# Turning the second chunk's y with VectorE and transfers instead of TensorE, and loading it first in the phase

## The chip, the cores and the metric

One NeuronCore of a Trainium2 chip. The metric is the device time of one execution in microseconds: the median of the runs, and for questions of where time goes, one execution that the hardware profiler recorded.

## The reference

An input x of 2048 tokens with 512 features goes through a normalization. Its result feeds two branches, whose outputs are multiplied and added to x:

```python
xn = _layernorm(x, axis=-1)
s = _A_ref(xn, A_wqkv, A_wo)                       # attention: 32 heads of 16, each query sees the 256 keys up to itself
g = _silu(_B_ref(xn, B_w1, B_b1, B_w2, B_b2))      # y = layernorm(xn); gelu(y @ w1 + b1) @ w2 + b2, with F = 1792
return x + s * g
```

Everything is float32.

## The kernel before

Matrix products are made of three passes: each operand is split into a high part that TensorE multiplies in one pass and a low rest, and high x high, high x low and low x high are added. A split is a cast (mostly on ScalarE) and a subtraction (on VectorE).

The kernel has two parts. Up to about 426 us it does the attention, with other work filled in between. Its results, not yet divided by the sums of the softmax, go to memory in `oT_d`, and the sums with them, as row `DH` of each head. Ten of the fourteen tiles of the hidden layer of the first 512 tokens are also made there, 2, 3 and 6 to 13; the last eight go to memory in `h_d`. Tiles 0 and 1 follow at its end.

The second part, which the change touches, runs over four chunks of 512 tokens. For chunk 0 (`c == 0` in the loop `for c in range(2)`) it runs over the 14 tiles of the hidden layer, in the order 2, 3, 0, 1, 4, 5, 6 to 13, by a counter `i`. For each tile, `activate` applies the gelu on ScalarE (`g`) and splits the result into `gh` and `gl`; `project` lets TensorE multiply these with w2 into `acc`, 12 matmuls a tile, of which every third reads `gl`. There are two buffers each of `gh` and `gl`. Tiles 4 and 5 are multiplied out here (`h`); the later ones come back from `h_d` (`hr`).

Beside this run over the tiles:

- the sums: `fetch_sums` loads them as `den`; VectorE inverts them in four parts; one transfer stores them (`rden_d`), and `load_o` brings back, for each of four groups, the attention (`or`) and the inverses spread over the partitions (`w<-rden_d` in the profile, since a w2 tile is used for them). VectorE multiplies the two and `split_o` splits the product (`ohl`);
- y of chunk 1: its four tiles of normalized x are loaded from `xn_d`, normalized once more (statistics on VectorE, a power on GpSimd, and here the normalization on VectorE), and, after the last `project`, turned by TensorE.

`end_chunk` adds the bias, applies the silu, and multiplies `ohl` with wo (`s`, 24 matmuls in the profile for each pair of token tiles). In chunk 0 it calls `between`, which puts the turning of y for chunk 1 before `s` of tiles 0 and 2: `y_transpose` makes four transposes of 128x128 into PSUM for each of four feature tiles, and splits the result into `yy`, the input of the hidden layer. Chunks 2 and 3 have their y turned in another way already: `turn_y` lets VectorE transpose a 128x512 tile in blocks of 32x32 and stores it in `z_d`, and `fetch_y` reads it back with four transfers for each feature tile, in runs of 32 elements, which puts the blocks in their places.

All transfers are issued by SyncE, one after the other, each waiting for what it needs; a wait holds up those behind it. Where `nc.sync.on` is set, they are issued in the order of the code; otherwise a scheduler may move them. Instructions of each other engine run in the order of the code. A transfer uses one of eight completion counters in turn, and its issue waits until the last one on its counter has landed.

Of the kernel before, what the change touches and what calls it, by code (L numbers as in the profile page):

```python
# [9 lines left out]
F32 = mybir.dt.float32  # L10
# [7 lines left out]
S, D, H, DH, WIN, F = 2048, 512, 32, 16, 256, 1792  # L18
P = 128
NCH = S // 512  # L20
NKB = S // P
KT = D // P
# [28 lines left out]
def mixer_kernel(ctx, tc, x, wqk, wv, wo, w1, b1, w2, b2, out):  # L51


    nc = SimpleNamespace(**{name: Ordered(tc, name) for name in ("tensor", "vector", "scalar", "gpsimd", "sync")})
# [3 lines left out]
    t2 = ctx.enter_context(tc.tile_pool(name="t2", bufs=5))  # L58
# [10 lines left out]
    def split(dst_hi, dst_lo, src, eng=None):  # L69

        (eng or nc.scalar.copy)(dst_hi, src)
        nc.vector.tensor_sub(dst_lo, src, dst_hi.bitcast(F32))
# [4 lines left out]
    def load(pool, tag, src, name, shape=(P, 512)):  # L77
        t = pool.tile(list(shape), F32, tag=tag, name=name)
        nc.sync.dma_start(t, src)
        return t  # L80
# [83 lines left out]
    def load_x(c, pools, name):  # L164
        return [load(*pools[i % len(pools)], x[512 * c + P * i: 512 * c + P * (i + 1), :], f"{name}_{c}_{i}")
                for i in range(4)]
# [19 lines left out]
    w_d = {"w1": dram.tile([P, NF * 512], F32, name="w1_d"), "w2": dram.tile([P, NF * 512], F32, name="w2_d"),  # L186
           "wo": dram.tile([P, 4 * 512], F32, name="wo_d")}
    g_d = dram.tile([NF, P, 512], F32, name="g_d")
    z_d = dram.tile([2, 4, P, 512], F32, name="z_d")
    mT_d = dram.tile([NQ, NCH, 32, P], F32, name="mT_d")  # L190


# [392 lines left out]
    mlp = {}  # L585
# [42 lines left out]
    def fetch(kind, f):  # L628

        nc.sync.dma_start(w_part(kind, 1, f).bitcast(F32), w_d[kind][:, 512 * f: 512 * (f + 1)])  # L630
# [9 lines left out]
    def y_steps(a, b):  # L640
        run(mlp["ln"][a:b])

    def y_transpose(c, kt, ps=None):
        ts = mlp["y"]
        if ps is None:
            ps = ps_yt.tile([P, 512], F32, tag="b", name=f"yt_{c}_{kt}")
        for i in range(4):
            nc.tensor.transpose(ps[:, P * i: P * (i + 1)], ts[i][:, P * kt: P * (kt + 1)], ident)
        split(mlp["yy"][0][kt], mlp["yy"][1][kt], ps)

    def hidden_mm(ps, f, k):
        kt, (a, b) = k // 3, PASSES[k % 3]
        nc.tensor.matmul(ps, w1_part(a, f)[:, P * kt: P * (kt + 1)], mlp["yy"][b][kt],
# [217 lines left out]
    wos = cp.tile([P, 2, 4, 512], F32R, name="wos")  # L871
    for f in range(W2_FIRST, NF):
        fetch("w2", f)
    for f in range(6, NF, 2):
        t = gp.tile([P, 2, 512], F32, tag="ohl", name=f"hr_{f}", bufs=4)
        nc.sync.dma_start(t, h_d[f - 6: f - 4].rearrange("f p t -> p f t"))
        ready.update({f: t[:, 0], f + 1: t[:, 1]})
    nc.sync.dma_start(b2s, bass.AP(tensor=b2.tensor, offset=b2.offset, ap=[[0, P], [1, 512]]))

    for g in range(4):  # L880
        fetch("wo", g)

    def load_y(c):
        if c > 1:
            return load_x(c, ((mlp["yp"], "y"),), "y")
        return [load(mlp["yp"], "y", xn_d[4 * c + i], f"y_{c}_{i}") for i in range(4)]

    def turn_y(c, tiles):

        for i in tiles:  # L890
            y = mlp["y"][i]
            nc.vector.transpose(y, y)
            nc.sync.dma_start(z_d[c - 2, i], y)

    def fetch_y(c, kt, dst):

        for k in range(4):
            at = z_d[c - 2, 0, 0, 128 * kt + 32 * k: 128 * kt + 32 * k + 32]
            nc.sync.dma_start(dst[32 * k: 32 * k + 32].rearrange("p (t j) -> p t j", j=32),
                              bass.AP(tensor=at.tensor, offset=at.offset, ap=[[512, 32], [32 * 512, 16], [1, 32]]))  # L900

    def fetch_sums():
        den = t2.tile([P, 512], F32, tag="t2", name="den")
        for g in range(4):
            nc.sync.dma_start(den[32 * g: 32 * g + 32], oT_d[g, :, DH].rearrange("a (c t) -> a c t", c=NCH))
        return den

    def load_o(c, g):

# [177 lines left out]
    for c in range(2):  # L1087
        accs = open_accs(c)
        gs, os_, hs, wanted = {}, [], {}, []
        made = ready if c == 0 else {}  # L1090

        def hidden(f):
            hs[f] = (ps_yt if c and f % 2 else ps_st).tile([P, 512], F32, tag="b", name=f"h_{c}_{f}")
            for k in range(3 * KT):
                hidden_mm(hs[f], f, k)

        def activate(f):
            if f in made and f in soon:
                gs[f] = made[f]
                return  # L1100
            src = made[f] if f in made else hs.pop(f)
            g = src if f in made and f < 2 else t2.tile([P, 512], F32, tag="t2", name=f"g_{c}_{f}")
            nc.scalar.activation(g, src, AF.Gelu_apprx_tanh, bias=b1s[:, f: f + 1])
            gs[f] = split_g(c, f, g, nc.scalar.copy)

        order = [2, 3, 0, 1, 4, 5, *range(6, NF)] if c == 0 else [*range(NF)]
        ahead = 2 + c
        for f in range(ahead if c else 0):
            hidden(f)
        o_from, o_late = (0, 0) if c else (8, 1)  # L1110
        nc.sync.on = c > 0
        for i in range(NF + 1):
            if i < NF:
                activate(order[i])
            if c and i in (1, 2, 6, 7):
                y_steps(6, 10)
            if c and i >= 10 and i < 14:
                second_y(i - 10)
            if c and i == 14:
                kept["w"] = bigp.tile([P, 768], F32R, tag="wb1", name="wsh")  # L1120
                combine_w(0)
            if c == 0:
                for kind, f in late_w[LATE[i]: LATE[i + 1]]:
                    settle(kind, f, nc.scalar.copy, nc.vector)
            if i >= 1:
                project(accs, [(order[i - 1], gs.pop(order[i - 1]))], order[0], order[-1])
            if i + ahead < NF and order[i + ahead] not in made and order[i + ahead] > 1:
                hidden(order[i + ahead])
            if c == 0:
                if i == 2:  # L1130
                    den = fetch_sums()
                if 4 <= i < 8:
                    nc.vector.reciprocal(den[:, P * (i - 4): P * (i - 3)], den[:, P * (i - 4): P * (i - 3)])
                    if i == 7:
                        nc.sync.dma_start(rden_d.rearrange("g a (c t) -> (g a c) t", c=NCH), den)
                if i == 4:
                    mlp["y"] = load_y(1)
                if i == 6:
                    mlp["ln"] = layernorm(mlp["y"], "C1", False)
                for back, (a, b) in enumerate(((0, 2), (2, 4), (4, 5), (5, 6), (6, 8), (8, 10))):  # L1140
                    if i == 6 + min(back, 5):
                        y_steps(a, b)
            else:
                steps2(i)
            k = i - o_from
            if 0 <= k - 2 - o_late < 4:
                os_.append(split_o(c, k - 2 - o_late, wanted[k - 2 - o_late][0]))
            if 0 <= k - 1 - o_late < 4:
                nc.vector.tensor_mul(wanted[k - 1 - o_late][0], *wanted[k - 1 - o_late])
            if 0 <= k < 4:  # L1150
                wanted.append(load_o(c, k))
            if c:
                if i in (2, 3, 7, 8):
                    turn_y(2 + i // 5, (0, 1) if i in (2, 7) else (2, 3))
                if i == 3:
                    mlp["y"] = load_y(3)
                    kept[0] = gated[:, 2:4]
                    kept[1] = bigp.tile([P, 2, 512], F32, tag="wb1", name="y2_21")
                    for kt in range(KT):
                        fetch_y(2, kt, kept[kt // 2][:, kt % 2])  # L1160
                if i in (8, 9):
                    for kt in (2 * i - 16, 2 * i - 15):
                        put("21" if kt > 1 else "11", kt % 2, kept[kt // 2][:, kt % 2])
                if i == 8:
                    fetch_second()
                if i == 12:
                    fetch_pair(0)
            if c and i in (0, 1, 5, 6):
                y_steps(5, 6)
        nc.sync.on = False  # L1170
        if c == 0:
            gated = bigp.tile([P, 4, 512], F32, tag="wa", name="gated")

        def between(i):
            if c == 0 and i in (0, 2):
                y_transpose(1, i)
                y_transpose(1, i + 1)
                if i == 2:
                    mlp["y"] = load_y(2)
            if c == 1 and i in (1, 2):  # L1180
                split_w(0, 2 * i - 2)
                split_w(0, 2 * i - 1)
        end_chunk(c, accs, os_, between)
        if c == 0:
            steps2(-1)
# [148 lines left out]
```

## Time and profile before

| | |
|---|---|
| time, median of 3 runs | 747.2 us (746.83 to 747.22) |
| the profiled execution | 747.81 us |
| its span, first to last instruction | 746.1 us |
| granted TensorE clock, mean | 0.998 |
| TensorE busy | 730.9 us |
| VectorE busy | 515.6 us |
| ScalarE busy | 436.9 us |
| chunk 0 of the second part, acc run of tiles 1 and 4 to 13 | 446.90 to 477.08 us |

In the profile all instructions have line 43, that of the helper which records them, so they are told apart by engine, operation and the names of their tiles: `acc<-w,gh` is a matmul of `project`, `yt<-ident,y` a transpose of `y_transpose`, `or<-or,w` the product of attention and inverses. PE is TensorE, PEld its weight loads, DVE VectorE, ACT ScalarE, POOL GpSimd, SPq the queue of SyncE. Times in a row of the timeline and the chain are start and length in us from the start of the span. A merged row of several instructions runs from the start of the first to the end of the last.

### The profile page before, as it was taken

How to read it: one execution, taken by the hardware profiler on the slowest of the kernel's cores; microseconds unless marked ns; L12 is line 12 of the kernel's file. 1: busy time of each engine (PE TensorE's matmuls, PEld its weight loads, DVE VectorE, ACT ScalarE, POOL GpSimd, SP SyncE). 2: the span in 40 equal slices, each digit the busy share in tenths (PEclk: the TensorE clock that was granted, in tenths of full speed). 3: DMA queues.
4: the chain of work that ended last, by engine and by line, in shares of the span. 5: the costliest groups of instructions: out<-in, count | busy, mean ns of one | idle time of the engine just before them, and what ended most of it. 6: DMA issues, size and time to landing. Idle time of an engine off the chain costs nothing.

```text
span 746.1 us, 18779 instructions
## 1 busy us (share of the span) xinstructions
PE 730.9 (98%) x7376; PEld 587.8 (79%) x7376; DVE 515.6 (69%) x789; ACT 436.9 (59%) x740; POOL 297.8 (40%) x644
## 2 busy tenths in 40 slices
PE   8999999999999999999999999999999999999997
PEld 7886777777778887777776688888888888888886
DVE  6886777877766678887773547856658755676643
ACT  7757767867667676778877745443544733442001
POOL 7313757757666555767867700030102000001102
PEclk9999999999999999999999999999999999999999
DMA  8633355667555625656725383356453322253611
GB/s 288 193 65 79 84 141 149 187 171 197 140 137 149 154 70 150 156 138 165 212 91 161 92 289 108 120 197 203 101 107 113 95 90 74 69 183 115 218 50 57
DMA packets 75001, 103.61 MB, mean 139 GB/s; under 512 B 28128, under 2 KB 28384, under 8 KB 74912
## 3 DMA queue, kind: packets, MB, share of 16 engines
q1 hardware_dynamic: 74912, 102.40, 48.4%
q8 instruction: 58, 0.95, 0.5%
q14 instruction: 31, 0.25, 0.1%
HBM read 53.48 MB, written 31.72 MB: 114 GB/s over the span
## 4 chain that ended last, share of the span: by engine, by line
PE 89%; ACT 5%; DVE 2%; POOL 2%; issue 1%; DMA 1%; SPq 0%; DVEq 0%; ACTq 0%; POOLq 0%
PE acc L43 20%; PE fb L43 19%; PE zo L43 11%; PE stb L43 9%; PE p L43 9%; PE s L43 6%; PE h L43 6%; PE xy L43 5%; ACT pt L43 4%; PE pv L43 3%; POOL pt L43 1%; DVE xy L43 1%; DMA x<-in_x_dram 1%; DVE mt L43 0%; ACT pjr L43 0%
## 5 line engine op out<-in xcount | busy, mean ns | idle before, releaser
L43 POOL TENSOR_SCALAR_AFFINE_SELECT pt<-pt 128x256 f32<-128x256 f32 x480 | 192.9, 426 | 133.8 <-ACT pt L43 131.2
L43 ACT ACTIVATE pt<-stb 128x768 f32<-128x768 f32 (+1 forms) x244 | 188.5, 773 | 62.6 <-PE stb L43 55.4
L43 DVE TENSOR_REDUCE mt<-xy 128x4 f32<-128x1024 f32 (+1 forms) x128 | 152.6, 1192 | 4.4
L43 DVE COPY_PREDICATED xy<-upper,zo 128x512 f32<-128x512 int32 x112 | 77.8, 695 | 70.5 <-PE xy L43 62.9
L43 POOL TENSOR_TENSOR xo<-xo,gated 128x512 f32<-128x512 f32 x15 | 19.9, 1330 | 218.3 <-DVE gated L43 214.2
L43 PE MATMUL fb<-xnT,wqb 64*128 64x512 f32 (+1 forms) x684 | 104.6, 397 | 0.2
L43 PE MATMUL zo<-pt,vt 128*17 128x128 f32 x2880 | 103.7, 275 | 0.3 <-POOL pt L43 0.3
L43 PE MATMUL stb<-qk 64*128 64x384 f32 (+1 forms) x488 | 97.2, 393 | 6.2 <-ACT pt L43 4.1
L43 PE MATMUL acc<-w,gh 128*128 128x512 f32 x320 | 98.6, 389 | 0.0
L43 PEld LDWEIGHTS stb<-qk 64*128 64x128 f32 x488 | 45.8, 183 | 51.6 <-ACT pt L43 46.4
L43 PEld LDWEIGHTS zo<-pt,vt 128*17 128x17 f32 x2880 | 67.5, 97 | 15.6 <-issue 6.4
L43 PEld LDWEIGHTS fb<-xnT,wqb 64*128 64x128 f32 (+1 forms) x684 | 64.6, 185 | 10.9 <-DVE pjr L43 1.4
L43 PEld LDWEIGHTS acc<-w,gh 128*128 128x128 f32 x320 | 60.1, 188 | 12.5
L43 PE MATMUL acc<-w,gl 128*128 128x512 f32 x160 | 62.4, 390 | 0.0
L43 PE MATMUL xy<-qk 64*128 64x256 f32 (+2 forms) x536 | 58.4, 291 | 0.2
L43 PEld LDWEIGHTS xy<-qk 64*128 64x128 f32 x536 | 46.7, 185 | 6.7 <-issue 3.1
L43 ACT COPY oraw<-zo 128x128 f32<-128x128 f32 x128 | 34.0, 266 | 29.4 <-PE zo L43 29.0
L43 ACT ACTIVATE gated<-acc 128x512 f32<-128x512 f32 x16 | 8.7, 595 | 63.4 <-DVE acc L43 63.4
L43 PE MATMUL s<-wos,ohl 128*128 128x512 f32 (+1 forms) x204 | 44.7, 377 | 0.0
L43 PEld LDWEIGHTS s<-wos,ohl 128*128 128x128 f32 x204 | 36.7, 188 | 7.0
L43 PEld LDWEIGHTS zo<-qk 64*128 64x128 f32 x448 | 38.6, 185 | 4.4 <-issue 1.4
L43 ACT COPY p<-p 128x512 f32<-128x512 f32 x21 | 12.3, 584 | 48.8 <-PE p L43 41.5
(193 smaller groups left out, 1235.1 us busy)
## 6 DMA issues: line engine op xcount, KB each, us to landing
qk<-sh SPq DMA_DIRECT2D x128, 128.0 KB
qk<-pjr SPq DMA_DIRECT2D x64, 128.0 KB
oT_d<-oraw SPq DMA_DIRECT2D x32, 256.0 KB
w_d<-in_w_dram SPq DMA_DIRECT2D x14, 512.0 KB
x<-in_x_dram SPq DMA_DIRECT2D x16, 256.0 KB
or<-oT_d SPq DMA_DIRECT2D x16, 256.0 KB
w<-rden_d SPq DMA_DIRECT2D x16, 256.0 KB
xo<-in_x_dram SPq DMA_DIRECT2D x16, 256.0 KB
```

What stands on the lines that cost most here:

```text
L43: r = issue(*args, **kwargs)
```

## The change

The second chunk's y is turned as that of the later chunks: VectorE transposes it in blocks of 32x32, four transfers store it, 16 bring it back in place, and ScalarE and VectorE split it in tiles 9 to 12 of the loop. `y_transpose` and its 16 matmuls go. y is loaded first, ahead of the hidden tiles; the sums are loaded after two of the four transfers of hidden tiles. The normalization of y moves from VectorE to ScalarE, its statistics from the counter 6 on to 3, and the transposes stand on VectorE ahead of the first inverse. The 16 loads of y stand in the queue ahead of the store of the inverses; all loads of attention come behind that store. The third chunk's y is loaded at counter 12 instead of in `between`. Transfers of chunk 0 keep the order of the code.

```diff
-    z_d = dram.tile([2, 4, P, 512], F32, name="z_d")
+    z_d = dram.tile([NCH - 1, 4, P, 512], F32, name="z_d")
...
-    def y_transpose(c, kt, ps=None):
...
+    mlp["y"] = [load(mlp["yp"], "y", xn_d[4 + i], f"y_1_{i}") for i in range(4)]
     for f in range(6, NF, 2):
         t = gp.tile([P, 2, 512], F32, tag="ohl", name=f"hr_{f}", bufs=4)
         nc.sync.dma_start(t, h_d[f - 6: f - 4].rearrange("f p t -> p f t"))
         ready.update({f: t[:, 0], f + 1: t[:, 1]})
+        if f == 8:
+            den = fetch_sums()
...
-        nc.sync.on = c > 0
+        nc.sync.on = True
...
             if c == 0:
-                if i == 2:
-                    den = fetch_sums()
+                if i == 3:
+                    mlp["ln"] = layernorm(mlp["y"], "C1", True)
+                    y_steps(0, 5)
+                if i == 4:
+                    y_steps(5, 10)
+                    turn_y(1, range(4))
                 if 4 <= i < 8:
                     nc.vector.reciprocal(den[:, P * (i - 4): P * (i - 3)], den[:, P * (i - 4): P * (i - 3)])
                     if i == 7:
                         nc.sync.dma_start(rden_d.rearrange("g a (c t) -> (g a c) t", c=NCH), den)
-                if i == 4:
-                    mlp["y"] = load_y(1)
-                if i == 6:
-                    mlp["ln"] = layernorm(mlp["y"], "C1", False)
-                for back, (a, b) in enumerate(((0, 2), (2, 4), (4, 5), (5, 6), (6, 8), (8, 10))):
-                    if i == 6 + min(back, 5):
-                        y_steps(a, b)
+                if i == 5:
+                    for kt in range(KT):
+                        fetch_y(1, kt, mlp["yy"][1][kt].bitcast(F32))
+                if 9 <= i < 13:
+                    split(mlp["yy"][0][i - 9], mlp["yy"][1][i - 9], mlp["yy"][1][i - 9].bitcast(F32))
+                if i == 12:
+                    mlp["y"] = load_y(2)
...
         def between(i):
-            if c == 0 and i in (0, 2):
-                y_transpose(1, i)
-                y_transpose(1, i + 1)
-                if i == 2:
-                    mlp["y"] = load_y(2)
```

More of the change, by code (lines that the diff above doesn't have):

```diff
@@ L641, in y_steps @@
         run(mlp["ln"][a:b])
-    def y_transpose(c, kt, ps=None):
[L644 to L649, printed above, removed]
     def hidden_mm(ps, f, k):
@@ L873, in mixer_kernel @@
         fetch("w2", f)
[L874 to L900, printed above, removed]
     def fetch_sums():
@@ L906, in fetch_sums, with load_y, turn_y, fetch_y @@
         return den
+    mlp["y"] = [load(mlp["yp"], "y", xn_d[4 + i], f"y_1_{i}") for i in range(4)]
+    for f in range(6, NF, 2):
+        t = gp.tile([P, 2, 512], F32, tag="ohl", name=f"hr_{f}", bufs=4)
+        nc.sync.dma_start(t, h_d[f - 6: f - 4].rearrange("f p t -> p f t"))
+        ready.update({f: t[:, 0], f + 1: t[:, 1]})
+        if f == 8:
+            den = fetch_sums()
+    nc.sync.dma_start(b2s, bass.AP(tensor=b2.tensor, offset=b2.offset, ap=[[0, P], [1, 512]]))
+    for g in range(4):
+        fetch("wo", g)
+    def load_y(c):
+        return load_x(c, ((mlp["yp"], "y"),), "y")
+    def turn_y(c, tiles):
+        for i in tiles:
+            y = mlp["y"][i]
+            nc.vector.transpose(y, y)
+            nc.sync.dma_start(z_d[c - 1, i], y)
+    def fetch_y(c, kt, dst):
+        for k in range(4):
+            at = z_d[c - 1, 0, 0, 128 * kt + 32 * k: 128 * kt + 32 * k + 32]
+            nc.sync.dma_start(dst[32 * k: 32 * k + 32].rearrange("p (t j) -> p t j", j=32),
+                              bass.AP(tensor=at.tensor, offset=at.offset, ap=[[512, 32], [32 * 512, 16], [1, 32]]))
     def load_o(c, g):
```

## The prediction

> **What bounds the kernel now.** I read the page first, then the chain that ended last, then the queue of transfers and VectorE around the change. TensorE is busy for 98% of the span.
>
> ```profile
> span 746.1 us, 18779 instructions
> PE 730.9 (98%) x7376; PEld 587.8 (79%) x7376; DVE 515.6 (69%) x789; ACT 436.9 (59%) x740; POOL 297.8 (40%) x644
> ```
>
> From 426 us on, the chain names nothing but TensorE. The columns are start and length in us, engine, tile and count:
>
> ```profile
> 446.90 30.18 PE acc L43 x132
> 477.95 5.46 PE s L43 x24
> 484.29 5.46 PE s L43 x24
> 489.74 10.88 PE h L43 x48
> ...
> 730.46 11.04 PE s L43 x60
> ```
>
> So whatever is taken off TensorE here moves the end by as much, and whatever holds it up pushes the end by as much. The 16 transposes of y that the change removes stand in the two gaps of this chain: 446.90 + 30.18 = 477.08 to 477.95 is 0.87 us, and 477.95 + 5.46 = 483.41 to 484.29 is 0.88 us.
>
> ```profile
> L43 PE MATMUL yt<-ident,y x16: 270/272/273, 476.9 to 484.0; 128*128 128x128 f32 x16
> ```
>
> **The change part by part.** *The transposes go:* −1.75 us, the two gaps. The row says 272 ns for one, but they overlap: eight take 0.87 us of the chain, 0.109 each. The Trainium skill (TensorE: Matmul & The Clock Gate, Part 4: PE-mode transpose) measures about 275 ns for one in a kernel; by that the sum would begin with 16 x 0.275 = −4.4 us. The duration agrees, but the chain is the row that the end follows.
>
> *VectorE and ScalarE before the sums.* The statistics now stand early. These are VectorE and ScalarE around them:
>
> ```profile
> 438.73 1.29 DVE L43 TENSOR_TENSOR w<-w 128x512 fp32r<-128x512 f32 x2
> 444.69 0.69 DVE L43 TENSOR_TENSOR gl<-g,gh 128x512 fp32r<-128x512 f32 x1 [4.67 <-ACT gh L43]
> 449.21 0.95 DVE L43 RECIPROCAL den<-den 128x128 f32<-128x128 f32 x1 [3.24 <-DMA den<-oT_d]
> 450.13 0.69 DVE L43 TENSOR_TENSOR gl<-g,gh 128x512 fp32r<-128x512 f32 x1
> 454.92 0.63 DVE L43 BATCH_NORM_STATS2 bnC<-y 128x6 f32<-128x512 f32 x1
> 456.48 0.67 DVE L43 TENSOR_TENSOR gl<-g,gh 128x512 fp32r<-128x512 f32 x1
> 497.71 2.94 ACT L43 ACTIVATE y<-y,shiftC_-1_7718,rsC_-1_7717 128x512 f32<-128x512 f32 x4 [1.10 <-DMA w<-rden_d]
> 506.14 1.30 DVE L43 STREAM_TRANSPOSE y<-y 128x512 f32<-128x512 f32 x2
> 461.54 1.39 POOL L43 TENSOR_TENSOR rsC<-veC,mhalf 128x4 f32<-128x4 f32 x1 [34.37 <-DVE veC L43]
> ```
>
> and two groups of the whole run (busy time, mean ns | idle before, releaser):
>
> ```profile
> L43 PEld LDWEIGHTS acc<-w,gl 128*128 128x128 f32 x160 | 30.0, 188 | 6.6 <-DVE gl L43 0.5
> L43 ACT CAST xnT<-yt 128x512 fp32r<-128x512 f32 x6 | 3.5, 608 | 2.3 <-PE yt L43 2.3
> ```
>
> VectorE is free from 440.0 to 444.7. Two statistics with their sums take 456.48 − 454.92 = 1.56, four 3.1: done at 443.2, inside that gap. GpSimd's power (1.39) ends at 444.7. After gl of tile 4 (444.69) and one weight half the shift comes at 446.0; four normalizations on ScalarE take 2.94, to 449.1; the transposes follow them one by one at 0.65, and the last ends at 449.8. The inverses start there instead of at 449.21, for the sums, third in the queue, have landed by then. So gl of tile 5 moves from 450.13 to 450.7 and ends at 451.4. The acc run from 446.90 is 11 blocks of 12 matmuls, for tile 1 and tiles 4 to 13. At 2.72 a block (24 matmuls take 5.44, as 48 take 10.88: 0.2267 each) tile 5 starts at 452.3 and reads gl in its third matmul. Some 1.2 us of cover remain, and this part costs nothing. Were the cover gone, each microsecond beyond it would be one of stall.
>
> The statistics no longer stand among the gl's from 454.92 on, which helps: the run of 30.18 is 132 x 0.2267 = 29.92 and 0.26 of waiting, and the weight loads' waits for gl are 0.5 us in the whole kernel. I book −0.25.
>
> *The queue.* SyncE issues in program order, and this is where the change can lose:
>
> ```profile
> 432.00 3.00 SPq L43 DMA_DIRECT2D hr<-h_d  x4
> 438.16 1.86 SPq L43 DMA_DIRECT2D wos<-wo_d  x4
> 440.90 4.50 SPq L43 DMA_DIRECT2D den<-oT_d  x4
> 445.44 2.22 SPq L43 DMA_DIRECT2D y<-xn_d  x4
> 458.65 0.32 SPq L43 DMA_DIRECT2D rden_d<-den  x1
> 460.63 1.19 SPq L43 DMA_DIRECT2D w<-rden_d  x2
> 537.84 0.91 SPq L43 DMA_DIRECT2D z_d<-y  x2
> 540.61 8.42 SPq L43 DMA_DIRECT2D xnT<-z_d  x16
> 549.07 0.96 SPq L43 DMA_DIRECT2D wr<-w_d  x2
> ```
>
> Before the inverses can be stored (rden_d), the changed program issues four stores of turned y and 16 small loads of them, and these loads wait until all four stores have landed. Before that, the transfer engines have work without a pause:
>
> ```profile
> 427.00:444.00 17.00, 17.00 (x96) 13.69 (x95) 7.95 (x13) 9.21 (x15) 0.17 (x1) 1.00 0.93 308
> 444.00:451.00 7.00, 7.00 (x32) 5.81 (x31) 3.08 (x5) 3.36 (x6) 0.00 (x0) 1.00 0.66 228
> 451.00:452.00 1.00, 1.00 (x6) 0.80 (x6) 1.00 (x2) 0.24 (x1) 0.00 (x0) 1.00 0.00 0
> ```
>
> (The last two columns are the engines' busy share and GB/s.) y moves to the front, but the bytes up to 451 are the same, so four stores issued from 447.7 to 449.8 queue behind some of them. From below: unqueued, the later stores go from 538.75 (537.84 + 0.91) to the first load at 540.61, 1.86 after their issue of 0.45 each; 449.8 + 2.3 = 452.1. From above: four times 256 KB, 1.05 MB, at 308 GB/s after 451.0, 454.4. I take 454.0, near the upper end, as the engines are still at 0.66. The 16 loads hold the queue for 549.07 − 540.61 = 8.46, so rden_d goes out at 462.5 (460.6 to 462.9) against 458.65, where it was not the queue but the last inverse that it waited for. The broadcast of the first inverses follows 460.63 − 458.65 = 1.98 later, at 464.4 (against 460.63). It is needed here, on VectorE:
>
> ```profile
> 464.52 1.00 DVE L43 TENSOR_SCALAR y<-y,mvC,rsC 128x512 f32<-128x512 f32 x2
> 467.25 0.69 DVE L43 TENSOR_TENSOR or<-or,w 128x512 f32<-128x512 f32 x1 [1.73 <-DMA w<-rden_d]
> 467.87 0.68 DVE L43 TENSOR_TENSOR gl<-g,gh 128x512 fp32r<-128x512 f32 x1
> 469.38 0.42 DVE L43 CAST ohl<-or 128x512 fp32r<-128x512 f32 x1
> 469.83 0.69 DVE L43 TENSOR_TENSOR ohl<-or,ohl 128x512 fp32r<-128x512 f32 x1
> 470.44 0.69 DVE L43 TENSOR_TENSOR or<-or,w 128x512 f32<-128x512 f32 x1
> 473.31 0.68 DVE L43 TENSOR_TENSOR gl<-g,gh 128x512 fp32r<-128x512 f32 x1
> 476.16 0.69 DVE L43 TENSOR_TENSOR ohl<-or,ohl 128x512 fp32r<-128x512 f32 x1
> ```
>
> Already before, VectorE stands 1.73 us at the first product of attention and inverse, until the broadcast lands at 467.25, 6.6 us after its issue. Queued behind this product on VectorE is gl of tile 11, which TensorE needs. How late may the product start? TensorE starts tile 13, the last, at 477.08 − 0.26 − 2.72 = 474.1 and reads its gl in the third matmul; with the weight load a matmul ahead, gl must be there 0.26 later, at 474.4. From the start of the first product to the end of that gl VectorE has, in the changed program, three products, two other gl's, two low halves of y and two of the attention, nine instructions at a pitch of 0.61 (469.83 to 470.44), two casts at 0.45 (469.38 to 469.83) and the gl itself, 0.69: 7.1 us. So 467.3 is the latest start without a stall; each microsecond beyond it is one on the chain.
>
> When does the broadcast land? From below as the sums did, which were issued by 445.40 and waited for until 449.21: 3.8, and with 0.6 of issue 4.4. From above as it did itself: 6.6, with a load of the attention shortly ahead of it, as now. I take 5.5, between the two, since the second broadcast no longer follows at its heels: one attention load comes between. It lands at 464.4 + 5.5 = 469.9, and TensorE stands 469.9 − 467.3 = 2.6 us over tiles 11 to 13.
>
> *The halves of y*, four casts of 0.61 on ScalarE and four subtractions on VectorE, move from the gate at 477 to 484 into tiles 9 to 13; those that stand after the first product are in the 7.1 us. The last ohl, at 476.16 before, is not read until nine matmuls (2.0 us) into the first s, which covers its part of the delay. The gate itself loses four of each in return. Loading the third chunk's y earlier is behind all this in the queue and waits for none of it.
>
> The sum: −1.75 − 0.25 + 2.6 = +0.6 us. The profiled execution took 747.81 us (span 746.1 and 1.7 around it), so 748.4 by its own time; the median of the runs, 747.2, lies 0.6 below it, which gives **747.8**.
>
> On the exchange as such the Trainium skill (VectorE: DVE Perf Modes, Rules for kernel authors) says to leave a 128x128 transpose to TensorE if PSUM will do as its destination; VectorE turns only blocks of 32x32, and the rest must be moved. By that rule the change loses. The rows bear it out in part: 1.75 us on TensorE are exchanged for 8.46 us of queue.
>
> **The rivals.** A measurement of this kernel tells apart about 0.2%, 1.5 us.
>
> *A, forecast, 0.48:* the stall eats the gain and a little more; 1.0 to 3.6 us of stall, −1.0 to +1.6, 746.2 to 748.8.
>
> *B, full gain, 0.18:* the stores are not queued (452.1) and the broadcast takes 4.4: 452.1 + 8.46 + 1.98 + 4.4 = 466.9, before 467.3. Then −2.0: 745.2. For it: y is loaded first and the engines' share is falling from 444. Against it: they run until 451.
>
> *C, slower, 0.30:* the broadcast keeps its 6.6 us and the stores land at 454.4. It lands at 454.4 + 8.46 + 1.98 + 6.6 = 471.4, a stall of 4.1, +2.1: 749.3. For it: it is the one measured time of this transfer in this place. It decides from a landing at 470.8 on (stall 3.5, +1.5). Within it stands a chance of 0.03 of a slowed clock: the granted clock reads 1.00 in the windows above, but no stall there is this long. If it fell to half for as long as the stall lasts, 4.1 us, 2.05 more are lost: 751.4. The Trainium skill (TensorE: Matmul & The Clock Gate, Part 1: The HAM clock gate) states such a halving after an idle window of about 3.4 us; no run here shows it.
>
> *D, 0.04:* the transposes cost TensorE more than their gaps show, up to their 272 ns: 16 x 0.272 = 4.35, and with the stall of 2.6 the end is 2.0 us earlier, 745.2. Against it: s starts at the modelled pitch right behind them.
>
> **How the numbers follow.** Faster by over 0.2% are B and D, most of them: 0.20. Slower is C and A's upper end: 0.33. Within, 0.47. The range 745.2 to 749.6 leaves out the slowed clock and the ends beyond B and C; A's own range is 746.2 to 748.8.
>
> **What would show it.** In the changed profile: s starting right after acc without a gap (−1.75); the 16 loads issued from 454.0 on; rden_d at 462.5; the first product on VectorE waiting for the broadcast until 469.9; TensorE's acc run no longer 30.18 but 32.5 us, with waits for gl. Wrong: acc at 29.9 (B), or loads that wait for something else, the statistics for y above all.

## The result, and the profile after

The changed kernel takes 751.7 us (median of 4 runs, 750.09 to 753.12) against 747.1 (746.83 to 747.22): a ratio of 1.0061, 95% interval 1.0041 to 1.0082. It is slower by 0.6%, and outside the predicted range. The profiled execution is the longest of the four, 753.12 us, 5.31 above that of before.

The page gives the span and TensorE's busy share:

```profile
span 751.4 us, 18806 instructions
PE 731.2 (97%) x7360; PEld 587.9 (78%) x7360; DVE 516.9 (69%) x790; ACT 440.1 (59%) x744; POOL 298.6 (40%) x644
```

16 matmuls fewer, and yet as much busy time as before (730.9): some matmuls took longer. The chain that ended last shows where (start, length, what; its main steps):

```profile
446.21 10.89 PE acc L43 x48
...
463.14 2.19 DMA rden_d<-den
465.36 6.75 DMA w<-rden_d
472.80 0.69 DVE gl L43
473.54 10.78 PE acc L43 x34
484.32 10.88 PE s L43 x48
495.20 10.88 PE h L43 x48
```

Before, this stretch was TensorE alone. Now the chain leaves TensorE for SyncE's queue, the store of the inverses and their first broadcast, and comes back to it through VectorE's gl. This execution reaches the acc run 0.69 us earlier than before did (446.21 against 446.90), ahead of anything that counts here; times are compared from the start of acc. From there to h it takes 48.99 us against 42.84, 6.15 more. The parts:

- the transposes: s follows acc without a gap (473.54 + 10.78 = 484.32) and is one run of 48. Both gaps are gone: −1.75, and the 0.26 of small waits inside acc with them.
- TensorE stands for gl of tile 11 (timeline of TensorE; in brackets the idle time before and what ended it):

```profile
467.81 0.61 PE L43 MATMUL acc<-w,gh 128*128 128x512 f32 x2
473.54 0.79 PE L43 MATMUL acc<-w,gl 128*128 128x512 f32 x1 [5.12 <-DVE gl L43]
```

- the 34 matmuls after that take 10.78 us where 34 x 0.2267 = 7.71 were due: 3.07 more. The stretches of 1 us have the reason, third from the right, the granted clock:

```profile
472.00:473.00 1.00, 0.00 (x0) 0.00 (x0) 0.81 (x2) 0.00 (x0) 0.00 (x0) 0.85 0.91 221
473.00:474.00 1.00, 0.46 (x1) 0.46 (x2) 1.00 (x2) 0.48 (x1) 0.00 (x0) 0.50 0.73 240
...
479.00:480.00 1.00, 1.00 (x5) 0.82 (x4) 1.00 (x3) 0.76 (x1) 0.00 (x0) 0.73 0.99 211
```

It falls to half near 472.7 (0.85 is 0.3 us at half) and is back near 479.5.

The sum, −1.75 − 0.26 + 5.12 + 3.07 = +6.18, is the 6.15 of the chain; less the head start of 0.69 it is 5.46, of which 5.31 are left between the two profiled executions at the end.

The long fall of the clock belongs to the profiled execution. Its mean granted clock is 0.994; the other three have 0.997, 0.998 and 0.998 (before: 0.998 to 1.000), and 6.84 us at half would alone bring the mean down to 0.9955. So the clock has a smaller part in the 4.6 us between the medians than the 3.07 here. How the rest of the 4.6 is made up, no trace shows.

The queue of SyncE and VectorE (timelines) show how the stall came about:

```profile
446.99 2.47 SPq L43 DMA_DIRECT2D z_d<-y  x4
454.76 8.29 SPq L43 DMA_DIRECT2D xnT<-z_d  x16
463.14 0.43 SPq L43 DMA_DIRECT2D rden_d<-den  x1
463.68 0.62 SPq L43 DMA_DIRECT2D or<-oT_d  x1
465.36 0.60 SPq L43 DMA_DIRECT2D w<-rden_d  x1
```

```profile
446.25 2.83 DVE L43 STREAM_TRANSPOSE y<-y 128x512 f32<-128x512 f32 x4 [0.89 <-ACT y L43]
449.84 0.63 DVE L43 TENSOR_TENSOR gl<-g,gh 128x512 fp32r<-128x512 f32 x1
456.09 0.94 DVE L43 RECIPROCAL den<-den 128x128 f32<-128x128 f32 x1
472.19 0.69 DVE L43 TENSOR_TENSOR or<-or,w 128x512 f32<-128x512 f32 x1 [7.85 <-DMA w<-rden_d]
```

The last inverse is ready at 457.0; its store waits in the queue until 463.14, behind the 16 loads, which themselves waited until 454.76 for the stores of turned y. VectorE then stands 7.85 us at the first product, and gl of tile 11 behind it.

### The profile page after: what moved, and what is told of

It is laid out like the page before. It is cut to its first block, busy times and chain, and to the rows that moved or that the text cites. A ratio compares the mean times of both kernels' runs of the same rounds, so it can differ in the third digit from the quotient of the medians.

```text
span 751.4 us, 18806 instructions
## 1 busy us (share of the span) xinstructions
PE 731.2 (97%) x7360; PEld 587.9 (78%) x7360; DVE 516.9 (69%) x790; ACT 440.1 (59%) x744; POOL 298.6 (40%) x644
## 4 chain that ended last, share of the span: by engine, by line
PE 86%; ACT 5%; DMA 3%; DVE 2%; POOL 2%; issue 1%; SPq 1%; DVEq 0%; ACTq 0%; POOLq 0%
PE acc L43 19%; PE fb L43 18%; PE zo L43 11%; PE p L43 9%; PE stb L43 9%; PE s L43 6%; PE h L43 6%; PE xy L43 5%; ACT pt L43 4%; PE pv L43 3%; POOL pt L43 1%; DMA qk<-sh 1%; DMA w<-rden_d 1%; DVE xy L43 1%; SPq L43 1%
## 5 line engine op out<-in xcount | busy, mean ns | idle before, releaser
L43 PE MATMUL acc<-w,gh 128*128 128x512 f32 x320 | 100.3, 395 | 0.0
```

Source lines behind the costliest of these rows:

```text
L43: r = issue(*args, **kwargs)
```

## The experiments

The first four share the runs of before with each other (median 746.95), so do e5 to e8 (747.03) and e9 and e10 (746.94).

**e1, four loads ahead instead of sixteen.**

```diff
                 if i == 5:
-                    for kt in range(KT):
+                    for kt in range(1):
                         fetch_y(1, kt, mlp["yy"][1][kt].bitcast(F32))
...
                 wanted.append(load_o(c, k))
+            if c == 0 and 0 <= k < KT - 1:
+                fetch_y(1, 1 + k, mlp["yy"][1][1 + k].bitcast(F32))
```

> The changed kernel, but only the four loads of the first feature tile of turned y stand in the queue ahead of the store of the inverses; the other twelve follow one by one behind the first three pairs of attention and inverses, and the four splits of y come one counter later. Nothing is left out. Theory (the queue ahead of the inverses is all that is wrong): the store waits for the last inverse again, 457.1; the first broadcast goes out at 459.3 and lands 6.7 later at 466.0, in time for tile 11; no stall, no fall of the clock, only the gain of the transposes: 745.2 to 745.9. Rival (turning y with VectorE and reading it back costs by itself, by VectorE's or ScalarE's load, or by the small loads holding up the broadcasts on the transfer engines): it stays above 747, with gaps in acc that end on something other than the first broadcast.

Measured: 752.18 us, ratio 1.0072 (1.0060 to 1.0085). A miss for the theory; the rival came true. The first half of the theory held; SyncE's queue and the first product on VectorE:

```profile
456.51 0.34 SPq L43 DMA_DIRECT2D rden_d<-den  x1
456.89 0.62 SPq L43 DMA_DIRECT2D or<-oT_d  x1
458.50 0.59 SPq L43 DMA_DIRECT2D w<-rden_d  x1
459.14 2.05 SPq L43 DMA_DIRECT2D xnT<-z_d  x4
461.29 1.92 SPq L43 DMA_DIRECT2D or<-oT_d  x1
...
472.06 2.87 SPq L43 DMA_DIRECT2D or<-oT_d  x1
474.98 0.58 SPq L43 DMA_DIRECT2D w<-rden_d  x1
```

```profile
463.70 0.69 DVE L43 TENSOR_TENSOR or<-or,w 128x512 f32<-128x512 f32 x1
```

The store goes out behind the last inverse, and the first product waits for nothing. But now the loads between the pairs hold up the pairs: an attention load that takes SyncE 0.6 us to issue stands up to 2.87. The chain shows how one of them was held: a small load issued at 465.73 lands 4.58 us later, ScalarE's cast of it and VectorE's work behind that come late, and the fourth attention load waits for VectorE until 472.89. What its issue waited for after that, up to 474.93, the profile doesn't name; a completion counter still taken by a small load would fit, but that isn't shown. The fourth broadcast goes out at 474.98 and takes 8.47 us. TensorE stands later instead (timeline):

```profile
476.56 0.50 PE L43 MATMUL acc<-w,gl 128*128 128x512 f32 x1 [2.96 <-DVE gl L43]
484.75 10.97 PE L43 MATMUL s<-wos,ohl 128*128 128x512 f32 x39 [3.57 <-DVE ohl L43]
```

**e2, twelve ahead, four behind the first pair** (the same edit with 3 for 1).

> As the first, with twelve of the sixteen loads ahead of the store, four behind the first pair. Theory: the store goes at 454.76 + 12 x 0.524 = 461.0, the first broadcast lands at 470.0, TensorE stands 3.0 us (5.12 less four loads of 0.52). If the clock falls only after longer stalls, 745.4 + 3.0 = 748.4; if it falls after 3.0 too, 751. Rival (the fall of the clock is not from the stall but from the many transfers then): clock 0.5 as in the changed kernel at the same time, 751.

Measured: 752.01 us, ratio 1.0067 (1.0055 to 1.0079). TensorE stood 3.3 us in all, near the expected 3.0, but that is luck. The store went out at 460.17 instead of 461.0 and the broadcast was waited for until 467.9, not 470.0, so the first pause is short. Then the second attention load stood 2.61 us in the queue behind the four small loads, and the second product came late with gl of tile 12. After this pause the clock was at half for 3.4 us. The median lies above both times of the theory, 748.4 and 751.

```profile
469.24 0.50 PE L43 MATMUL acc<-w,gl 128*128 128x512 f32 x1 [0.69 <-DVE gl L43]
474.85 0.50 PE L43 MATMUL acc<-w,gl 128*128 128x512 f32 x1 [2.60 <-DVE gl L43]
```

**e3, the pause filled with matmuls.**

```diff
+            if c == 0 and i == 12:
+                idle = ps_yt.tile([P, 512], F32, tag="b", name="idle")
+                for k in range(18):
+                    nc.tensor.matmul(idle, wos[:, 0, 0, 0:P], wos[:, 0, 0], start=(k == 0), stop=(k == 17))
             if i >= 1:
                 project(accs, ...
```

> The changed kernel, with 18 matmuls of wo with itself (4.1 us) into a PSUM bank that nobody reads, on TensorE ahead of tile 11: they stand in the time in which TensorE waited. Work is added, none is left out. Theory (the pause makes the clock fall to half, 2.65 us): the pause is 1.0 us, the granted clock stays 1.00, acc goes on at 0.227 per matmul, the time falls by 2.6 to about 749. Rival (the matmuls were slow for another reason, as the traffic of the transfers, or the fall costs nothing in the other runs): matmuls of 0.43 again, or time unchanged at 751 to 752.

Measured: 750.53 us, ratio 1.0048 (1.0036 to 1.0060); profiled execution 750.52, against 753.12 without the extra matmuls. Adding work made the profiled execution shorter:

```profile
467.59 4.24 PE L43 MATMUL idle<-wos 128*128 128x512 f32 x18
...
479.14 0.50 PE L43 MATMUL acc<-w,gl 128*128 128x512 f32 x1 [1.01 <-DVE gl L43]
```

The 18 matmuls cover the pause: gl of tile 11 follows at 472.22 with hardly a wait. The wait of 1.01 is a different one, of tile 13, for the third broadcast; in the changed kernel the slow clock had hidden it. The granted clock reads 1.00 in every stretch from 440 to 490, and its mean is 0.999 or 1.000 in all five executions: with TensorE kept at work the clock doesn't fall. From the start of acc to s it takes 35.73 us against 38.11, 2.38 less, so in this pair of executions the fall was worth less than its 3.07. Between the profiled executions the 2.6 expected are there. Between the medians it is 1.2, and the two sets of times overlap, as the other executions of the changed kernel had less of a fall to lose.

**e4, the first attention load ahead of the 16 loads.**

```diff
                 if i == 5:
+                    first_o = load(t2, "t2", oT_d[0, :, 0:DH, 0:512], "or_0_0")
                     for kt in range(KT):
                         fetch_y(1, kt, mlp["yy"][1][kt].bitcast(F32))
...
-                wanted.append(load_o(c, k))
+                wanted.append(load_o(c, k, None if c or k else first_o))
```

> The changed kernel, with the load of the first attention tile moved ahead of the 16 loads, where the queue stands for the stores anyway; the first broadcast then has no transfer of 256 KB just ahead of it. Theory (the broadcast takes 3.7 to 4.7 by itself and 6.7 because it stands behind the attention load on the same transfer engines): issued at 465.36 as before, landing at 469.1 to 470.1, stall 2.1 to 3.1 without a fall of the clock: 747.5 to 748.5. Rival (a broadcast of rows just stored takes 6.7 by itself): landing at 472.1, time as before, 751.7.

Measured: 748.80 us, ratio 1.0028 (1.0017 to 1.0038). SyncE's queue, VectorE and TensorE:

```profile
453.27 8.29 SPq L43 DMA_DIRECT2D xnT<-z_d  x16
463.79 0.62 SPq L43 DMA_DIRECT2D w<-rden_d  x1
```

```profile
468.73 0.69 DVE L43 TENSOR_TENSOR or<-or,w 128x512 f32<-128x512 f32 x1 [4.49 <-DMA w<-rden_d]
```

```profile
470.08 0.50 PE L43 MATMUL acc<-w,gl 128*128 128x512 f32 x1 [1.76 <-DVE gl L43]
477.35 0.50 PE L43 MATMUL acc<-w,gl 128*128 128x512 f32 x1 [1.34 <-DVE gl L43]
```

Without an attention load just ahead of it the broadcast is waited for until 4.9 us after its issue, not 6.8. (It also went out earlier, for the stores of turned y had landed by 453.27 in this execution.) The first stall shrinks to 1.76 and the clock stays at 1.00. A second one of 1.34 appears, for the third broadcast, and with it the time lies just above the expected 747.5 to 748.5.

**e5, the third chunk's y later** (e4, with `load_y(2)` moved from counter 12 back into `between`).

> The kernel of e4 (first attention load ahead of the 16 loads), with the third chunk's y loaded where it was before the change, ahead of s of token tile 2, and not at counter 12. Theory (the four loads of the third chunk, 1 MB, share the transfer engines with the last pairs of attention and inverses, and cause the second gap of 1.34 us in e4): the third broadcast lands by 474, the second gap goes, the first of 1.8 stays, 748.8 - 1.3 = 747.5. Rival (the pairs pace themselves at about 2 us each, whatever else is loaded): both gaps as in e4, 748.8.

Measured: 751.17 us, ratio 1.0046 (1.0033 to 1.0059). A miss that tests nothing of the theory: in `between` SyncE's transfers aren't held in the order of the code, and the scheduler put two of these loads ahead of the 16 and two ahead of the first broadcast.

```profile
451.62 0.99 SPq L43 DMA_DIRECT2D y<-in_x_dram  x2
...
463.13 0.43 SPq L43 DMA_DIRECT2D rden_d<-den  x1
463.61 0.93 SPq L43 DMA_DIRECT2D y<-in_x_dram  x2
```

TensorE stood 4.38 us at tile 11 once more, and the clock fell. Whether the third chunk's loads slow the last pairs stays open.

**e6, all sixteen behind the pairs.**

```diff
                 if i == 5:
-                    for kt in range(KT):
-                        fetch_y(1, kt, mlp["yy"][1][kt].bitcast(F32))
-                if 9 <= i < 13:
-                    split(mlp["yy"][0][i - 9], ...
-                if i == 12:
-                    mlp["y"] = load_y(2)
+                    first_o = load(t2, "t2", oT_d[0, :, 0:DH, 0:512], "or_0_0")
...
+            if c == 0 and i == 11:
+                for kt in range(KT):
+                    fetch_y(1, kt, mlp["yy"][1][kt].bitcast(F32))
...
         def between(i):
+            if c == 0 and i < 2:
+                for kt in (2 * i, 2 * i + 1):
+                    split(mlp["yy"][0][kt], mlp["yy"][1][kt], mlp["yy"][1][kt].bitcast(F32))
+            if c == 0 and i == 2:
+                mlp["y"] = load_y(2)
```

> All 16 loads of turned y issued behind the last pair of attention and inverses, y split at the gate (two feature tiles ahead of s of token tile 0, two ahead of tile 1), third chunk's y loaded where it was before the change, first attention load early as in e4. Statistics, normalization, transposes and their stores stay as in the changed kernel; nothing is left out. Theory (only the order of the queue was wrong): inverses stored at 457.1, first broadcast lands at 464 to 466, no gap in acc, s right behind it, the gain of the transposes is kept: 745.2 to 746.0 and every run within 0.5 us. Rival (the turned y comes too late for the first hidden tile of chunk 1, or the transposes were worth less than 1.75): h starts later than s ends, or a time of 746.5 to 748.

Measured: 745.06 us (744.75 to 745.89), ratio 0.9975 (0.9964 to 0.9985): faster than both kernels, by the 2.0 us that the prediction booked for the change without its queue. (One of the eight runs lies 0.8 above the median, where 0.5 was expected.) The chain, and SyncE's queue:

```profile
446.11 29.92 PE acc L43 x132
476.03 10.99 PE s L43 x48
487.03 10.88 PE h L43 x48
```

```profile
456.97 0.33 SPq L43 DMA_DIRECT2D rden_d<-den  x1
...
464.91 13.23 SPq L43 DMA_DIRECT2D xnT<-z_d  x16
```

acc takes 132 x 0.2267 = 29.92 exactly, s and h follow without a gap. The 16 loads now take 13.23 us of the queue, behind the broadcasts, and nothing that TensorE needs soon waits for them. But the edit moves more than these loads: the first attention load goes ahead as in e4, the splits of y leave the tiles for the gate, and the scheduler placed the third chunk's loads earlier than intended, from 451.82 on, while the queue stood for the last inverse. How much of the time needs each of these wasn't tried.

**e7, the sixteen loads issued by GpSimd** (`nc.gpsimd.dma_start` in `fetch_y` for this chunk, at the same place).

> The changed kernel, with the 16 loads of turned y issued by GpSimd instead of SyncE, at the same place of the code. Theory (it is SyncE's queue that delays the inverses, not the transfers themselves): the store goes at 457.1, the first broadcast goes out at 459.3 and lands at 464 to 466 while the small loads still run; no first gap; the last pairs still meet the third chunk's loads: 745.5 to 747.5. Rival (the small loads hold up the broadcasts on the transfer engines, as they were held up by them in e1, or GpSimd takes much longer for each): the splits of y wait on ScalarE, gl with them, 749 or more.

Measured: 749.27 us, ratio 1.0028 (1.0017 to 1.0039): the rival's range. SyncE's queue, then TensorE:

```profile
457.07 0.32 SPq L43 DMA_DIRECT2D rden_d<-den  x1
459.87 0.60 SPq L43 DMA_DIRECT2D w<-rden_d  x1
```

```profile
473.76 0.50 PE L43 MATMUL acc<-w,gl 128*128 128x512 f32 x1 [2.48 <-DVE gl L43]
```

VectorE's second product:

```profile
472.42 0.69 DVE L43 TENSOR_TENSOR or<-or,w 128x512 f32<-128x512 f32 x1 [1.42 <-DMA y<-in_x_dram]
```

The queue is freed as expected, and the first stall gone. But the small loads still run among the pairs: ScalarE waits 2.17 and 1.56 us for two of them, VectorE waits 1.44 for ScalarE, and the second product starts 11.2 us after its broadcast went out (461.18). The stall moves to tile 12, behind this product. Another queue gives back 2.4 us of the 4.6 lost, another order (e6) all of it and the gain.

**e8, the transposes back in e6.**

```diff
         def between(i):
+            if c == 0 and i in (0, 2):
+                for k in range(2):
+                    turned = ps_yt.tile([P, 512], F32, tag="b", name=f"turned_{i}_{k}")
+                    for j in range(4):
+                        nc.tensor.transpose(turned[:, P * j: P * (j + 1)], ident, ident)
```

> The kernel of e6, with 16 transposes of the identity into PSUM put back on TensorE where the kernel before had those of y (eight ahead of s of token tile 0, eight ahead of tile 2); nobody reads them, so their halves cost nothing on other engines. Theory (they cost their two gaps, 0.109 us each): 1.75 above e6. Rival D of the prediction (they cost up to 272 ns each): up to 4.35 above e6.

Measured: 746.57 us, ratio 0.9993 (0.9985 to 1.0002): 1.51 above e6, 0.094 for each transpose. They cost about their gaps.

**e9, broadcasts that begin with 16 rows.**

```diff
-    rden_d = dram.tile([4, 8, S], F32, name="rden_d")
+    rden_d = dram.tile([4, 8, 2, S], F32, name="rden_d")
...
-                                       ap=[[S, 8], [0, DH], [1, 512]]))
+                                       ap=[[S, 16], [0, DH // 2], [1, 512]]))
...
-                        nc.sync.dma_start(rden_d.rearrange("g a (c t) -> (g a c) t", c=NCH), den)
+                        for r in range(2):
+                            nc.sync.dma_start(rden_d[:, :, r].rearrange("g a (c t) -> (g a) c t", c=NCH), den)
```

> The changed kernel, with the inverses stored twice (two transfers of 256 KB), so that the broadcast's pattern in memory begins with 16 rows of 8 copies instead of 8 rows of 16 copies; the attention loads and all else stay. In the changed kernel the transfer engines read 0.41 to 0.48 busy while only attention and broadcasts were on the way, half of the 16. Theory (a broadcast that begins with 8 rows uses 8 engines, and its landing time is the queue on these 8): its 4.4 us behind the attention load fall to about 2.2, it lands near 470.3 instead of 472.1, the stall is near 3.3; later broadcasts come sooner too; 748.5 to 751 as the clock falls or not. Rival (the time is that of reading the same few rows many times): landing and time as in the changed kernel, 751.7.

Measured: 750.74 us, ratio 1.0049 (1.0037 to 1.0062). From the chain:

```profile
465.77 4.67 DMA w<-rden_d
```

4.67 where the changed kernel had 6.75, behind an attention load as there: 2.1 less, as expected. TensorE stood 3.0 us, and the clock fell as long as before (10.79 for 34 matmuls). Between the profiled executions 1.70 us reach the end, between the medians 0.95. The Trainium skill (DMA: Bandwidth & Descriptors, Rules for kernel authors) says that a transfer uses no more engines than the size of its slowest dimension allows, and to put a multiple of 16 there; the landing agrees, but the engines' busy share doesn't show it: it is 0.39 to 0.49 from 465 to 470 here too. Storing the rows twice also halves how often each is read, so the rival isn't ruled out, and why the broadcast got faster stays open.

**e10, both e4 and e9.**

> The kernel of e4 (first attention load ahead of the 16 loads) with the same double store. Theory: the first broadcast goes out at 464.2 and lands at 467.0 (4.9 in e4 less 2.2), so the first gap of 1.76 falls to about 0.4, the second of 1.34 goes: 745.5 to 746.5. Rival: as e4, 748.8.

Measured: 748.02 us, ratio 1.0019 (1.0010 to 1.0028). Half a hit. The second gap is gone. The first stayed at 1.78: the broadcast took 3.83, but it went out at 464.90, behind the second store (chain, then TensorE's timeline):

```profile
464.90 3.83 DMA w<-rden_d
```

```profile
470.10 0.50 PE L43 MATMUL acc<-w,gl 128*128 128x512 f32 x1 [1.78 <-DVE gl L43]
```

## Why the prediction was wrong

*Transposes, −1.75:* right. s starts at the end of acc, and e8 puts them at 1.51. Rival D (4.35) is out.

*Statistics, normalization and turning at no cost:* right. The last transpose ended at 449.08 and gl of tile 5 at 450.47, which from the start of acc is as predicted (449.8 and 451.2 on the scale of before, against 449.8 and 451.4); TensorE waited for nothing there. The waits of 0.26 in acc are gone.

*The mechanism:* right. The store of the inverses stands behind the loads of turned y, and the first product waits for the broadcast with gl of tile 11 behind it. e6 turns this order round, with three smaller moves beside it, and gets the whole gain.

*The landing of the first broadcast, 469.9:* the first step that failed, by 2.9 us. Measured from the start of acc, the loads began 1.45 later than booked (454.76 + 0.69 against 454.0, later even than the upper end of 454.4); the hold of the queue was right (8.38 against 8.46); store to broadcast took 0.24 more; and the broadcast 6.75 instead of 5.5, near its 6.6 of before. Its price had been taken midway to the sums' 4.4, since no second broadcast follows at once. But the second broadcast went out only 1.31 us behind the first (466.67 against 465.36), so that was no ground for less than 6.6. The runs have it at 4.9 without an attention load ahead (e4), at 6.75 behind one, and behind one but with small loads instead of the next pair on its heels at 5.5 (e2) and at most 5.2 (e1): both what goes ahead and what follows seem to count. The late start of the loads is in part this execution's: after the same transfers they began, on the scale of before, at 455.45 here, but at 454.77 in e3, 454.56 in e9 and 454.36 in e1. Why isn't settled.

*The latest start of the product, 467.3:* right within 0.5. That is 466.6 here; the product started 5.6 later, and TensorE stood 5.12. It stood at tile 11, whose gl comes right behind the product; the bound had come from tile 13, which waits as well when the clock stays up (1.01 in e3).

*The stall, 2.6:* so 5.12, and the forecast's own rule, a microsecond for each one late, held.

*The clock:* the second step that failed. The sum put it at nothing; the prediction gave it a chance of 0.03, and 751.4 with it. That this is nearly the measured 751.7 is partly luck: its stall of 4.1 and its 2.05 for the clock were 5.12 and 3.07 in the profiled execution, which took 753.12, and in the other executions the clock fell less. The 3.07 came from 6.84 us at half, of which only 0.84 lay in the pause. e3 shows that the pause is the cause. Against it spoke only that no stall of that length had been seen, and that is no evidence.

So rival C was the right case, and its chance of 0.30 and that of its clause on the clock were too small: the 6.6 was the only measured time of this transfer in this place, and should have been the value taken instead of the bound.

Rival B's full gain exists, but not in this order of transfers. The rule of the Trainium skill that the prediction weighed (VectorE: DVE Perf Modes, Rules for kernel authors: leave such a transpose to TensorE) was right for this kernel, and not for e6, where TensorE sets the end and the transfers have nothing waiting behind them.

## What to carry to other kernels

When work moves to a queue that issues in order, ask first who is served behind it, and put what the bound engine needs soon ahead of what it needs late: in e6, with the 16 loads behind the pairs (and a few other moves), the loss of 4.6 us becomes a gain of 2.0. Another issuing engine didn't replace the order: the work behind the small loads still waited for them (e7). Price a longer stall of TensorE with the clock as well: of the seven pauses of 2.48 us and more in these runs six were followed by a fall, of those up to 1.78 none.

## What the runs showed of the hardware

The clock didn't need a long pause. In e7 TensorE stood 2.48 us, and it fell (granted clock third from the right):

```profile
474.00:475.00 1.00, 1.00 (x4) 0.80 (x4) 0.97 (x3) 1.00 (x1) 0.00 (x0) 0.66 0.96 305
...
477.00:478.00 1.00, 1.00 (x5) 0.79 (x4) 0.64 (x1) 0.00 (x0) 0.00 (x0) 0.64 0.79 238
```

From 474.32 to 477.72, 3.40 us at half, while TensorE was back at work from 473.76 on; in the changed kernel it was 6.84, from 472.70 to 479.54, twice that. The length of the pause doesn't set this: e9 paused for 3.01 us and had 6.82 at half (471.06 to 477.88), e5 for 4.38 and had 3.42 (472.38 to 475.80). What goes with it in these four is when TensorE was back at work: 0.56 us before the fall in e7 and 0.12 behind it in e5, but 0.84 and 0.82 behind it in the changed kernel and in e9. After e4's pauses of 1.76 and 1.34 it did not fall, nor after e1's of 2.96, though after e1's of 3.57 (the 39 matmuls of s there take 10.97, some 2 us more than 39 x 0.2267). So whether the clock falls isn't a matter of the length alone either. The Trainium skill (TensorE: Matmul & The Clock Gate, Part 1: The HAM clock gate) states a free-running window of about 3.4 us and a fall after an idle one. The lengths of 3.4 and 6.8 us agree with such a window, and a pause that falls across two of them would explain e1; but a window that was idle for 2.48 of its 3.4 us sufficed in e7.
